# An attention and mixture-of-experts kernel: one subtraction in two instructions, new planner costs, and full-width products for one chunk in nine

## The chip, the cores and the metric

The kernel runs on one core of a Trainium2 chip. The metric is the device time of one execution in microseconds (us); the kernel before takes 906.83 us as the median of three runs (902.57 to 909.19). The engines that the text speaks of are TensorE (PE in the rows; PEld is its weight load), VectorE (DVE), ScalarE (ACT), GpSimd (POOL) and SyncE (SP), which issues most transfers. Each works through a queue of its own in order; semaphores tie them together.

## The reference

Attention over 4 batches, 8 heads, 1152 keys and 64 columns, with the queries averaged in pairs (576 per batch and head), and then a mixture of 8 experts of which each token takes two:

```python
q_pool = q.reshape(B, H, S // 2, 2, D).mean(axis=3)
scores = scale * np.matmul(q_pool, k.transpose(0, 1, 3, 2))
scores = scores - np.max(scores, axis=-1, keepdims=True)
attn = np.exp(scores)
attn = attn / (np.sum(attn, axis=-1, keepdims=True) + 1e-09)
x = np.matmul(attn, v)                       # then tokens x 512
noisy = x @ w_gate + np.log1p(np.exp(x @ w_noise)) * noise
top2 = np.argpartition(-noisy, 2, axis=1)[:, :2]   # softmax of the two: weights
out[mask] += top2_w[mask, k, None] * (np.maximum(x[mask] @ w1[e], 0) @ w2[e])
```

## The kernel before

**Attention.** The work is cut into 16 pairs (two batches of one head). A pair has 9 chunks of 128 queries; chunk 4 is mixed: its first 64 queries are of the first batch and its last 64 of the second. Three chunks make a segment, so there are 48 segments, and the middle segment of each pair (g = 1) holds the mixed chunk. A segment goes through 9 steps of 128 keys. Two steps make a unit, 216 in all.

For a unit, TensorE computes the scores (`score`, lines 342 and 343, two matmuls for each step and batch), ScalarE takes the exponential into a pair of buffers as 32-bit numbers `pf` (`exp`, line 350), and then P is split: the upper 16 bits of each number, read in place as bf16, are the high half `ph`, and `pl = pf - ph`, as f16, is the low half (`p_lo`, line 354). This subtraction is done by either GpSimd or VectorE, 140 and 76 times. The product with V (`pv`, line 370) takes both halves: for each step and chunk, three matmuls in which P is the stationary operand and V, with a column of ones that gives the row sum, is the moving one: ph with 65 columns of V's high half, ph with 64 of V's low half, pl with 65 of the high half. For the mixed chunk each of the three is done twice, with 64 stationary columns each, one time with each batch's V, into partitions 0 to 63 and 64 to 127 of the same PSUM columns. After the ninth step `evac` divides by the row sum (lines 381 to 383) on VectorE, and ScalarE and VectorE split the result into two f16 halves (388, 390).

Ahead of a pair's scores stand its loads, the splits of K, Q and V into halves (lines 281 on VectorE, 284 on ScalarE), transposing transfers, differences of keys (`kd`, line 291) and a pass that finds each query's maximum (scores on TensorE, line 297; ScalarE 305; VectorE 311 and 320). The PSUM has two wide tiles for scores and four banks; the banks serve the maximum pass, the products with V and the routing by turns. P has six buffer pairs.

**The planner.** The order of the attention's instructions on every queue is set at build time by `Plan`: each piece of work is an `op` with an engine, a booked duration, a due key, what it depends on and which buffers it takes. The planner walks a clock forward, holds an in-order queue for each engine (`LAT` is booked from a result to its reader, `GAP` between two works on an engine), and always writes out the op that can start first; within 0.25 us it takes the one with the smaller key. Works that use the SBUF port which VectorE and GpSimd share (`port=True`) are not booked at the same time. Where two engines are given, as for `p_lo`, it takes the one that would end first. The booked numbers decide the order and the split between engines; the chip runs that order with its own durations. For a step of P x V the op books 0.29 us, whether the segment is a middle one or not.

**After the attention.** The routing of the first 1152 tokens (`Route.steps`, lines 640 to 790: transposes, gate products, some 60 small VectorE instructions, then GpSimd's scatters, line 99) is planned inside the attention. The routing of the second half starts as segments end; its pieces that the plan hasn't placed by the attention's end are woven into `Moe.early`, which runs two experts on their first 256 tokens (matrix products 927 and 948, relu and its correction 936 and 937, weight splits 872 and 874). Then `Moe.run` takes the experts at full width, each after its tokens were fetched by a transposing transfer.

## Time and profile before

| | |
|---|---|
| median of three runs | 906.83 us (902.57 to 909.19) |
| the profiled execution | 906.73 us, of which 904.9 us span |
| TensorE busy, matmuls | 825.2 us (91%), 8686 matmuls |
| VectorE busy | 539.1 us (60%) |
| ScalarE busy | 445.4 us (49%) |
| GpSimd busy | 354.5 us (39%) |
| mean granted clock of TensorE | 0.975 |
| P x V (line 370) | 47 to 458 us |

A busy time is the union of an engine's instructions; matmuls overlap in a pipeline, so a row with 0.19 us for a matmul doesn't mean that the next starts only then, and how long a run of them takes is read from their start times. Shares over the whole span mix two parts: attention, where all engines work, and the experts, where TensorE is nearly always busy and the others aren't.

### The profile page before, as it was taken

The page shows a single profiled execution, that of the slowest core. Times are in us where ns is not written, and L with a number is a line of the kernel's source. Part 1 is how long each engine was busy: PE and PEld are TensorE (multiplying, and loading weights), DVE is VectorE, ACT ScalarE, POOL GpSimd, SP SyncE. Part 2 cuts the span into 40 slices and gives each one's busy share as a digit, 9 for nine tenths or more (in the row PEclk, how much of TensorE's full clock was granted, in tenths as well). Part 3 has the DMA queues.
Part 4 walks back from the last instruction along what each step waited for, and adds up shares of the span by engine and source line. Part 5 has one row for each costly group of instructions (what it writes and reads, how often), then busy time and mean ns, then how long its engine had stood idle before and what let it go on. Part 6 is the DMA issues. An engine that isn't in the chain of part 4 may idle for free.

```text
span 904.9 us, 21011 instructions
## 1 busy us (share of the span) xinstructions
PE 825.2 (91%) x8686; PEld 540.2 (60%) x8686; DVE 539.1 (60%) x1257; ACT 445.4 (49%) x663; POOL 354.5 (39%) x317
## 2 busy tenths in 40 slices
PE   3799899999999699789987799999999999999995
PEld 0367666767677566567774455757465565647542
DVE  4988887988899898898888133334323241422200
ACT  4678787767776466676534132333333332322310
POOL 4347577666762468755306501020211202020132
PEclk9889999999999799999999899999999999999998
DMA  8897986898699649574387936273836437281143
GB/s 195 204 245 166 202 212 178 179 216 182 153 219 184 172 106 215 130 204 98 109 166 258 255 43 165 65 220 84 209 71 172 108 106 176 71 212 22 24 51 44
DMA packets 213636, 137.79 MB, mean 152 GB/s; under 512 B 150304, under 2 KB 183584, under 8 KB 213536
## 3 DMA queue, kind: packets, MB, share of 16 engines
q1 hardware_dynamic: 204896, 116.33, 53.4%
q0 software_dynamic: 8640, 20.08, 11.4%
q8 instruction: 69, 1.13, 0.5%
q14 instruction: 31, 0.25, 0.1%
HBM read 62.14 MB, written 35.44 MB: 108 GB/s over the span
## 4 chain that ended last, share of the span: by engine, by line
PE 69%; DVE 17%; issue 6%; POOL 3%; DMA 3%; ACT 1%; SPq 1%; ACTq 0%; POOLq 0%; DVEq 0%
PE pss L927 21%; PE psm L948 20%; PE psm L370 13%; PE psm L297 6%; PE pss L342 5%; PE pss L343 5%; DVE pl L354 3%; DVE rd L311 3%; POOL xg L99 2%; DVE vv L281 2%; DVE mx L320 1%; DMA kr<-in_k_dram 1%; DVE kd L291 1%; DMA xT<-xg 1%; DVE rt L700 1%
## 5 line engine op out<-in xcount | busy, mean ns | idle before, releaser
L354 POOL TENSOR_TENSOR pl<-pf 128x768 f16<-128x768 f32 x140 | 223.8, 1610 | 148.6 <-ACT pf L350 140.4
L350 ACT ACTIVATE pf<-pss 128x768 f32<-128x768 f32 x216 | 173.9, 811 | 75.8 <-PE pss L343 67.1
L370 PE MATMUL psm<-vv,pf 128*128 128x65 f16 (+2 forms) x2880 | 188.8, 199 | 4.7 <-DVE vv L281 3.4
L370 PEld LDWEIGHTS <-pf 128*128 128x128 bf16 (+1 forms) x2880 | 156.0, 101 | 60.0 <-issue 20.5
L99 POOL DMA_INDIRECT out_dram<-y,mti x40 | 62.6, 1566 | 326.3 <-ACT y L953 316.6
L370 PE MATMUL psm<-vv,pl 128*128 128x65 f16 (+1 forms) x1440 | 176.3, 195 | 1.8 <-DVE pl L354 1.8
L343 PE MATMUL pss<-qt,kt 66*128 66x384 f16 (+1 forms) x576 | 149.9, 289 | 0.1
L342 PE MATMUL pss<-qt,kt 128*128 128x384 f16 (+1 forms) x576 | 149.3, 288 | 0.6 <-ACT pf L350 0.5
L937 DVE SCALAR_TENSOR_TENSOR hl<-pss,hh 128x640 f16<-128x640 f32 (+2 forms) x68 | 50.2, 738 | 159.0 <-ACT hh L936 159.0
L370 PEld LDWEIGHTS <-pl 128*128 128x128 f16 (+1 forms) x1440 | 127.9, 103 | 5.8 <-issue 3.7
L948 PE MATMUL psm<-wh,hl 128*128 128x512 f16 x320 | 121.3, 379 | 0.0
L948 PE MATMUL psm<-wl,hh 128*128 128x512 f16 x320 | 121.3, 379 | 0.0
L948 PE MATMUL psm<-wh,hh 128*128 128x512 f16 x320 | 121.3, 379 | 0.0
L936 ACT ACTIVATE hh<-pss 128x640 f16<-128x640 f32 (+2 forms) x68 | 43.2, 635 | 131.8 <-PE pss L927 131.8
L948 PEld LDWEIGHTS <-hh 128*128 128x128 f16 x640 | 62.4, 98 | 73.3
L311 DVE CUSTOM_DVE_ANT_0 rd<-psm,rd 128x512 f32<-128x512 f32 x144 | 96.7, 682 | 14.2 <-ACT rd L305 13.3
L305 ACT ACTIVATE rd<-psm 128x512 f32<-128x512 f32 x144 | 85.8, 597 | 36.9 <-PE psm L297 17.5
L953 ACT ACTIVATE y<-psm,mg 128x512 f32<-128x512 f32 x40 | 27.5, 687 | 151.2 <-issue 77.3
L297 PE MATMUL psm<-kt,qt 128*128 128x512 f16 (+3 forms) x320 | 78.3, 321 | 21.1 <-DVE mx L311 8.5
L927 PE MATMUL pss<-xT,fh 128*128 128x320 f16 (+1 forms) x448 | 85.7, 308 | 4.9 <-DMA xT<-xg 4.9
L354 DVE TENSOR_TENSOR pl<-pf 128x768 f16<-128x768 f32 x76 | 85.3, 1133 | 2.4 <-ACT pf L350 2.3
L927 PE MATMUL pss<-xT,wh 128*128 128x320 f16 (+1 forms) x448 | 83.4, 303 | 0.0
(157 smaller groups left out, 1170.3 us busy)
## 6 DMA issues: line engine op xcount, KB each, us to landing
xg<-zt SPq DMA_DIRECT2D x40, 260.0 KB, 5.3
kr<-in_k_dram SPq DMA_DIRECT2D x32, 288.0 KB, 3.7
vr<-in_v_dram SPq DMA_DIRECT2D x16, 576.0 KB, 4.6
kr<-in_moe_w_dram SPq DMA_DIRECT2D x17, 512.0 KB, 4.6
qr<-in_moe_w_dram SPq DMA_DIRECT2D x16, 512.0 KB, 4.3
kn<-in_moe_w_dram SPq DMA_DIRECT2D x16, 512.0 KB, 3.6
qr<-in_q_dram SPq DMA_DIRECT2D x31, 256.0 KB, 3.5
vr<-in_moe_w_dram SPq DMA_DIRECT2D x15, 512.0 KB, 5.3
```

Of the source, the lines that this page charges most:

```text
L99: i = nc.gpsimd.indirect_dma_start(out=out, out_offset=bass.IndirectOffsetOnAxis(ap=idx, axis=0), in_=src, in_offset=None, **kw)
L297: s.nc.tensor.matmul(ps[r, o:o + m.shape[1] * P], s.G.buf["qt", i][:, c, r], m, start=True, stop=True)
L305: s.nc.scalar.activation(s.G.buf["rd", i, c], s.G.buf["D", i, c], AF.Relu)
L311: s.nc.vector.tensor_tensor_reduce(out=rd, in0=s.G.buf["S", i, c], in1=rd, scale=1.0, scalar=-3.0e38, op0=ALU.add, op1=ALU.max, accum_out= ...
L342: mm(ps[:, a, o:o + w], kt[:, hh * NK + kc, :], qf[:, q0:q0 + w], start=True, stop=False)
L343: mm(ps[:, a, o:o + w], kt2[0:66, hh * NK + kc, :], qf2[0:66, q0:q0 + w], start=False, stop=True)
L350: s.nc.scalar.activation(s.parts(u)[0], s.G.buf["ps", u][:, :, 0:SG], AF.Exp, scale=0.125 / (IN_SCALE * IN_SCALE))
L354: (s.nc.vector if eng == "DVE" else s.nc.gpsimd).tensor_sub(pl, pf, ph)
L370: mm(ps[o:o + m, ci, 0:w], src[:, t % 2, ci * P + o:ci * P + o + m], vv[:, hh * NK + kc, a:b], start=st, stop=last and src is pl, skip_gro ...
L927: nc.tensor.matmul(ps[:, i, 0:N], w[:, dc, f * P:(f + 1) * P], xT[:, 2 * dc + x, i * N:(i + 1) * N], start=(n == 0), stop=(n == 11))
L937: s.nc.vector.scalar_tensor_tensor(hl, ps, 0.0, hh, op0=ALU.max, op1=ALU.subtract)
L948: nc.tensor.matmul(ps, h[:, f, b * P:(b + 1) * P], w[:, f, :], start=(n == 0), stop=(n == 23))
```

## The change

Three things are changed. `p_lo` on GpSimd becomes two instructions, one for each step of the unit (128 x 384 in place of 128 x 768); on VectorE it stays one. In `pv` the mixed chunk's three matmuls are done with all 128 stationary columns for both batches: with the first batch's V into the chunk's own PSUM columns, of which partitions 0 to 63 are used, and with the second batch's into 64 spare columns of the bank (`other`, columns 195 to 258), of which partitions 64 to 127 are used; the row sum needs no second copy, since it doesn't depend on V. `evac` has one more VectorE instruction for these 64 x 64 values, and its scratch columns move by 8. And the planner's booked durations are changed in nearly all ops. The core of the diff:

```diff
-    LAT = {"PE": 0.25, "ACT": 0.1, "DVE": 0.1, "POOL": 0.12, "SP": 4.0}
-    GAP = {"PE": 0.0, "ACT": 0.04, "DVE": 0.03, "POOL": 0.03, "SP": 0.05}
+    LAT = {"PE": 0.25, "ACT": 0.14, "DVE": 0.11, "POOL": 0.12, "SP": 4.0}
+    GAP = {"PE": 0.0, "ACT": 0.01, "DVE": 0.01, "POOL": 0.02, "SP": 0.05}
...
     def p_lo(s, u, eng):
         pf, ph, pl = s.parts(u)
-        (s.nc.vector if eng == "DVE" else s.nc.gpsimd).tensor_sub(pl, pf, ph)
+        if eng == "DVE":
+            s.nc.vector.tensor_sub(pl, pf, ph)
+            return
+        for a in range(2):
+            s.nc.gpsimd.tensor_sub(pl[:, a], pf[:, a], ph[:, a])
+
+    def other(s, n):
+        return s.G.buf["pv", n][:, 195:259]
...
-            parts = [(0, 0, 64), (1, 64, 64)] if c == 4 else [(int(c > 4), 0, P)]
             for src, a, b, w in ((ph, 0, 65, 65), (ph, 65, 129, 64), (pl, 0, 65, 65)):
-                for hh, o, m in parts:
+                for hh in (0, 1) if c == 4 else (int(c > 4),):
                     st = kc == 0 and ci == 0 and src is ph and a == 0
-                    mm(ps[o:o + m, ci, 0:w], src[:, t % 2, ci * P + o:ci * P + o + m], vv[:, hh * NK + kc, a:b],
+                    o = s.other(n) if hh and c == 4 else ps[:, ci]
+                    x = min(w, o.shape[1])
+                    mm(o[:, 0:x], src[:, t % 2, ci * P:ci * P + P], vv[:, hh * NK + kc, a:a + x],
                        start=st, stop=last and src is pl, skip_group_check=True)
...
             nc.vector.tensor_mul(xa, ps[:, :, 0:64], r.to_broadcast([P, 3, 64]))
+            if g == 1:
+                nc.vector.tensor_mul(xa[64:P, 1], s.other(n)[64:P], r[64:P, 1].to_broadcast([64, 64]))
             return
...
-            ex[u] = op("ACT", 0.82, 2 * u + 0.2, lambda u=u: s.exp(u), deps=[sc], take=[("pt", ("pt", u))], give=[("ps", u)])
-            pls[u] = op((("POOL", 1.5), ("DVE", 0.9)), 0, 2 * u + 2, lambda eng, u=u: s.p_lo(u, eng), deps=[ex[u]], port=True)
+            ex[u] = op("ACT", 0.71, 2 * u + 0.2, lambda u=u: s.exp(u), deps=[sc], take=[("pt", ("pt", u))], give=[("ps", u)])
+            pls[u] = op((("POOL", 1.43), ("DVE", 0.87)), 0, 2 * u + 2, lambda eng, u=u: s.p_lo(u, eng), deps=[ex[u]], port=True)
...
-                done.append(op("PE", 0.29, t + 8, lambda n=n, kc=kc: s.pv(n, kc), deps=[pls[t // 2]] + vdone[i] + done[-1:],
+                done.append(op("PE", 0.375 if n % 3 == 1 else 0.28, t + 8, lambda n=n, kc=kc: s.pv(n, kc), deps=[pls[t // 2]] + vdone[i], after=done[-1] if done else None,
```

The last pair of lines also lets a step of P x V be booked right behind the step before it on TensorE, where before it was booked only after that step's result time.

What the planner makes of it can be read from the built order. On TensorE, a middle segment's step around the mixed chunk (psm is the segment's bank, pf and pl the two halves of P, vv is V with its column of ones). Before, after a full-width chunk:

```order
L370 LDWEIGHTS pf_119
L370 MATMUL psm_66<-vv_128,pf_119 128x64
L370 LDWEIGHTS pl_120
L370 MATMUL psm_66<-vv_128,pl_120 128x65
L370 LDWEIGHTS pf_119
L370 MATMUL psm_66<-vv_128,pf_119 64x65
L370 LDWEIGHTS pf_119
L370 MATMUL psm_66<-vv_128,pf_119 64x65
L370 LDWEIGHTS pf_119
L370 MATMUL psm_66<-vv_128,pf_119 64x64
L370 LDWEIGHTS pf_119
L370 MATMUL psm_66<-vv_128,pf_119 64x64
```

And such a place now:

```order
L378 LDWEIGHTS pf_109
L378 MATMUL psm_66<-vv_128,pf_109 128x64
L378 LDWEIGHTS pl_110
L378 MATMUL psm_66<-vv_128,pl_110 128x65
L378 LDWEIGHTS pf_109
L378 MATMUL psm_66<-vv_128,pf_109 128x65
L378 LDWEIGHTS pf_109
L378 MATMUL psm_66<-vv_128,pf_109 128x64
L378 LDWEIGHTS pf_109
L378 MATMUL psm_66<-vv_128,pf_109 128x64
L378 LDWEIGHTS pf_109
L378 MATMUL psm_66<-vv_128,pf_109 128x64
```

The number of matmuls in the step is the same, twelve; the first number of a matmul's size is the count of output partitions, and all are 128 now. On GpSimd, the start of the attention before (qs is the sum of query pairs):

```order
L436 TENSOR_TENSOR qs_100<-qr 128x576 x2
L354 TENSOR_TENSOR pl_116<-pf_115 128x768
L354 TENSOR_TENSOR pl_118<-pf_117 128x768
L354 TENSOR_TENSOR pl_120<-pf_119 128x768
L436 TENSOR_TENSOR qs_100<-qr 128x576
```

And now:

```order
L446 TENSOR_TENSOR qs_100<-qr 128x576
L358 TENSOR_TENSOR pl_110<-pf_109 128x384 x2
L358 TENSOR_TENSOR pl_118<-pf_117 128x384 x2
L358 TENSOR_TENSOR pl_110<-pf_109 128x384 x2
L358 TENSOR_TENSOR pl_112<-pf_111 128x384 x2
L446 TENSOR_TENSOR qs_100<-qr 128x576
```

Each unit is two rows on end, and which units GpSimd takes has changed; over the whole program it takes 139 units where it took 140, and VectorE 77 where it took 76. On VectorE, the end of the attention before, from the last subtraction on (r and psm close a segment, wl is the low half of an expert's weight, ru and rt are the routing, hl is the correction of a relu):

```order
L390 TENSOR_TENSOR xr_84<-psm_67,xr_84 128x3x64
L381 TENSOR_SCALAR r<-psm_68 128x3
L382 RECIPROCAL r<-r 128x3
L383 TENSOR_TENSOR psm_68<-psm_68,r 128x192
L390 TENSOR_TENSOR xr_85<-psm_68,xr_85 128x3x64
L874 SCALAR_TENSOR_TENSOR wl_8041<-qr,wh_8040 128x1024
L675 TENSOR_SCALAR ru_7839<-psm_67 128x48
L680 SCALAR_TENSOR_TENSOR rt_8096<-ru_7839 128x24
L682 TENSOR_SCALAR rt_8096<-rt_8096 128x24
L937 SCALAR_TENSOR_TENSOR hl<-pss_64,hh 128x256
```

And now, from the close of the last segment on:

```order
L389 TENSOR_SCALAR r<-psm_67 128x3
L390 RECIPROCAL r<-r 128x3
L391 TENSOR_TENSOR psm_67<-psm_67,r 128x192
L400 TENSOR_TENSOR xr_85<-psm_67,xr_85 128x3x64
L884 SCALAR_TENSOR_TENSOR wl_8196<-qr,wh_8195 128x1024
L947 SCALAR_TENSOR_TENSOR hl<-pss_64,hh 128x256
L884 SCALAR_TENSOR_TENSOR wl_8196<-kn,wh_8195 128x1024
L947 SCALAR_TENSOR_TENSOR hl<-psm_66,hh 128x256
L884 SCALAR_TENSOR_TENSOR wl_8196<-kr,wh_8195 128x1024
L685 TENSOR_SCALAR ru_8008<-psm_68 128x48
L690 SCALAR_TENSOR_TENSOR rt_8287<-ru_8008 128x24
L692 TENSOR_SCALAR rt_8287<-rt_8287 128x24
```

The first row of the second half's routing stands behind one weight split before, and behind three weight splits and two relu corrections now.

## Rows read from the trace of the kernel before

**Rows 1.** Busy us (and instructions) by engine in five stages; granted clock, DMA.

```profile
47.00:300.00 253.00, 237.64 (x3759) 175.89 (x3759) 216.13 (x467) 189.31 (x293) 157.83 (x100) 0.99 0.88 196
300.00:400.00 100.00, 84.04 (x1234) 61.81 (x1233) 90.59 (x230) 61.47 (x95) 70.39 (x68) 0.93 0.68 166
400.00:458.00 58.00, 55.43 (x981) 44.45 (x978) 49.49 (x85) 37.32 (x55) 22.28 (x13) 0.97 0.45 102
458.00:516.00 58.00, 45.71 (x410) 31.12 (x407) 38.72 (x222) 20.21 (x36) 27.16 (x44) 1.00 0.82 242
516.00:905.00 389.00, 377.25 (x2208) 216.84 (x2207) 110.78 (x178) 111.82 (x148) 59.35 (x73) 0.98 0.48 109
```

The columns are start and end, length, PE, PEld, DVE, ACT, POOL, then the granted clock of TensorE, the share of DMA and GB/s.

**Rows 2.** Chain of waits from 47 to 458 us, shares by engine and line.

```profile
by line: PE psm L370 27.6%; PE psm L297 11.5%; PE pss L342 10.4%; PE pss L343 10.3%; issue 8.2%; DVE pl L354 5.3%; DVE rd L311 4.7%; DVE vv L281 3.1%; DVE mx L320 2.3%; DVE kd L291 1.8%; DMA kr<-in_k_dram 1.2%; DVE rt L700 1.2%; DVE kn L281
```

**Rows 3.** Timeline of TensorE, a middle segment's step: start, us, engine, line, operation.

```profile
137.09 0.23 PE L370 MATMUL psm<-vv,pf 128*128 128x65 f16 x2
...
137.28 0.26 PE L370 MATMUL psm<-vv,pf 128*64 128x65 f16 x4
...
137.50 0.23 PE L370 MATMUL psm<-vv,pf 128*128 128x65 f16 x2
...
137.60 0.38 PE L297 MATMUL psm<-kd,qt 128*128 128x512 f16 x1
```

**Rows 4.** The same timeline, an ordinary step of P x V.

```profile
139.71 0.22 PE L370 MATMUL psm<-vv,pf 128*128 128x65 f16 x2
...
139.99 0.33 PE L342 MATMUL pss<-qt,kt 128*128 128x384 f16 x1
```

**Rows 5.** Shortest, middle and longest ns of a line's instructions; last, one small GpSimd group.

```profile
L354 POOL TENSOR_TENSOR pl<-pf x140: 1458/1469/2361, 29.2 to 449.3; 128x768 f16<-128x768 f32 x140
L354 DVE TENSOR_TENSOR pl<-pf x76: 942/950/2784, 29.2 to 456.3; 128x768 f16<-128x768 f32 x76
L281 DVE SCALAR_TENSOR_TENSOR kn<-kr,kn x32: 741/1084/3662, 5.0 to 381.6; 128x576 f16<-128x576 f32 x32
L281 DVE SCALAR_TENSOR_TENSOR vv<-vr,vv x17: 745/1473/2618, 33.0 to 437.4; 128x1152 f16<-128x1152 f32 x15, 128x576 f16<-128x576 f32 x2
L291 DVE TENSOR_TENSOR kd<-kt x32: 404/733/2456, 9.7 to 391.7; 128x512 f16<-128x512 f16 x32
L598 POOL IOTA ev<- 128x8 f32 x1 | 0.1, 133 | 0.0
```

**Rows 6.** Timelines of VectorE and GpSimd at 65 us.

```profile
65.12 2.02 DVE L281 SCALAR_TENSOR_TENSOR qn<-qs,qn 128x576 f16<-128x576 f32 x1
...
65.06 1.47 POOL L354 TENSOR_TENSOR pl<-pf 128x768 f16<-128x768 f32 x1 [2.23 <-ACT pf L350]
```

**Rows 7.** Pieces of the whole chain of waits: start, us, what (twelve such).

```profile
99.68 2.22 DVE pl L354
...
440.78 2.15 DVE pl L354
```

**Rows 8.** Waits from 60 to 440 us; then two groups of the page.

```profile
POOL pl L354 <- ACT pf L350: 126.1, 74, 6.8
...
PE psm L297 <- DVE mx L311: 13.4, 11, 4.7
...
L354 POOL TENSOR_TENSOR pl<-pf 128x768 f16<-128x768 f32 x140 | 223.8, 1610 | 148.6 <-ACT pf L350 140.4
L350 ACT ACTIVATE pf<-pss 128x768 f32<-128x768 f32 x216 | 173.9, 811 | 75.8 <-PE pss L343 67.1
```

**Rows 9.** The chain of waits from 440 to 520 us.

```profile
458.48 0.38 DVE psm L383
...
479.95 0.99 POOL xg L99
...
509.11 7.25 DMA xT<-xg
```

**Rows 10.** Small route steps on VectorE, 440 to 520 us: count, busy us, mean ns.

```profile
L700 DVE SCALAR_TENSOR_TENSOR rt<-rt,rt 128x24 f32<-128x24 f32 x18 | 3.1, 172 | 0.1
```

More of the change, by code (lines that the diff above doesn't have):

```diff
@@ L418, in pairs @@
             for h, c in enumerate(hs):
-                hi = op("ACT", 0.69, k(50, 90) + 4 * h, lambda i=i, c=c: s.hi(B["kn", i][:, c, 0:D], B["kr", i][:, c], scale),
+                hi = op("ACT", 0.58, k(50, 90) + 4 * h, lambda i=i, c=c: s.hi(B["kn", i][:, c, 0:D], B["kr", i][:, c], scale),
                         deps=[lk[h]], take=[("kn", ("kn", i)), ("kt", ("kt", i))] if h == 0 else (), after=hi)
-                lo = op("DVE", 0.73, k(48, 90) + 4 * h,
+                lo = op("DVE", 0.67, k(48, 90) + 4 * h,
                         lambda i=i, c=c: s.lo(B["kn", i][:, c, D:], B["kr", i][:, c], scale, B["kn", i][:, c, 0:D]),
@@ L444, in q_hi @@
                          B["qs", i][:, c, None, :].to_broadcast([P, m, 2, D]), 0.5 * scale)
-                hi = op("ACT", 0.2 + 0.96 * f, k(44, 91) + 8 * p * x, q_hi, deps=[a])
+                hi = op("ACT", 0.1 + 0.96 * f, k(44, 91) + 8 * p * x, q_hi, deps=[a])
                 t = op("SP", 1.35, k(43, 91) + 8 * p * x, lambda i=i, c=c: s.transpose(B["qt", i][:, c], B["qn", i][:, c]), deps=[hi], lat=2.7,
@@ L460, in pairs @@
                     c = 3 * g + ci
-                    mm = op("PE", 0.44, k0 + 3 * ci, lambda i=i, c=c: s.max_mm(i, c),
+                    mm = op("PE", 0.62 if c == 4 else 0.43, k0 + 3 * ci, lambda i=i, c=c: s.max_mm(i, c),
                             deps=[df[h] for h in w] + [q],
                             take=[("bank", ("D", i, c)), ("bank", ("S", i, c))], give=[("kd", i)])
-                    rl = op("ACT", 0.61, k0 + 3 * ci + 0.5, lambda i=i, c=c: s.max_relu(i, c), deps=[mm],
+                    rl = op("ACT", 0.48, k0 + 3 * ci + 0.5, lambda i=i, c=c: s.max_relu(i, c), deps=[mm],
                             take=[("rd", ("rd", i, c))], give=[("D", i, c)])
-                    red.append(op("DVE", 0.78, k0 + 3 * ci + 1, lambda i=i, c=c: s.max_red(i, c), deps=[rl],
+                    red.append(op("DVE", 0.67, k0 + 3 * ci + 1, lambda i=i, c=c: s.max_red(i, c), deps=[rl],
                                   give=[("S", i, c), ("rd", i, c)]))
-                rest = op("PE", 0.17, k0 + 5, lambda i=i, g=g: s.max_rest(i, g), deps=red, take=[("bank", ("R", i, g))])
-                red.append(op("DVE", 0.57, k0 + 7, lambda i=i, g=g: s.rest_red(i, g), deps=[rest], give=[("R", i, g)]))
+                rest = op("PE", 0.39 if g == 1 else 0.17, k0 + 5, lambda i=i, g=g: s.max_rest(i, g), deps=red, take=[("bank", ("R", i, g))])
+                red.append(op("DVE", 0.47, k0 + 7, lambda i=i, g=g: s.rest_red(i, g), deps=[rest], give=[("R", i, g)]))
                 allred += red
@@ L483, in pairs @@
             for h, c in enumerate(vs):
[L484 removed]
+                hi = op("ACT", 0.1 + 0.96 / len(vs), b + 3 * h, lambda i=i, c=c: s.hi(B["vv", i][:, c, 0:D], B["vr", i][:, c], scale),
                         deps=[lv], take=[("vv", ("vv", i))] if h == 0 else (), after=hi)
[L486 removed]
+                vdone[i].append(op("DVE", 0.08 + 1.2 / len(vs), b + 3 + 6 * h,
                                    lambda i=i, c=c: s.lo(B["vv", i][:, c, 65:129], B["vr", i][:, c], scale, B["vv", i][:, c, 0:D]),
```

16 lines of the change are left out of this document (7 added, 9 removed).

## The prediction

> **What bounds the kernel now.** I first cut the span into stages by what runs in them. From 516 us on, TensorE is busy for 377 of 389 us with the experts' matrix products, at a granted clock of 0.98 [rows 1]; nothing of the diff touches that code, so these 389 us stay. What the change can move lies before. All P x V products (line 370) lie between 47 and 458 us, and in these 411 us three engines are all nearly full: between 47 and 300 us TensorE is busy for 237.6, VectorE for 216.1 and GpSimd for 157.8 of 253 us [rows 1]. From 300 to 400 us, where the routing of the first half of the tokens runs on VectorE, VectorE has 90.6 of 100 us and TensorE falls to 84.0, its granted clock to 0.93. So no single engine is the bound: the reader should see a ring of three in-order queues that wait for each other by turns.
>
> The chain of waits over 47 to 458 us says which of them ends last: P x V (L370) 27.6%, the other three TensorE lines together 32.2%, VectorE's lines 18.4% as far as the row goes (pl 5.3, rd 4.7, vv 3.1, mx 2.3, kd 1.8, rt 1.2; kn is cut off behind), and 8.2% in which nothing is named [rows 2]. GpSimd's subtraction is not on the row, and GpSimd waits 126.1 us for the exponential in the 380 us from 60 to 440, the largest wait of that stretch, while TensorE waits 13.4 us for VectorE's running maximum [rows 8]. A slower GpSimd is thus hidden; a shorter P x V and a VectorE that is held up less are not.
>
> **The mixed chunk's products.** A step of ordinary P x V is nine matmuls; the one from 139.71 to 139.99 us takes 0.28 us, 0.031 each [rows 4]. A step of a middle segment has twelve, six of them with 64 stationary columns, and takes from 137.09 to 137.60, 0.51 us [rows 3]. Inside it the six half-wide ones take 0.22 (137.28 to 137.50), 0.037 each, so half the columns are not cheaper; the rest of the difference stands at the two changes of width. With 128 columns throughout, twelve times 0.031 is 0.37 us. The count of matmuls stays, the 64-column forms disappear (the order shows them as 128-wide rows). There are 16 middle segments of 9 steps, 144 in all, so TensorE has 144 x 0.14 = 20 us less to do. That is not yet time. All of P x V is 288 x 0.28 + 144 x 0.51 = 154 us, and the chain holds 27.6% of 411 = 113 us of it, 0.74. I take 0.74 x 20 = **-15 us**; the bounds are 0 (each step was waiting anyway) and -20.
>
> **The subtraction in halves.** One GpSimd instruction over 768 elements takes 1.458 us at least, and the same on VectorE 0.942 [rows 5]. The two do not overlap: at 65.06 us GpSimd starts one and ends at 66.53; VectorE's subtraction for q starts at 65.12 and takes 2.02 us [rows 6] where the shortest of that shape in line 281 takes 0.741 [rows 5]. It stood still for 1.28 us, until GpSimd's instruction was nearly over. The same shows in the spread of VectorE's own forms: kd from 0.404 to 2.456 us, kn from 0.741 to 3.662, pl from 0.942 to 2.784 [rows 5]. On the chain I find twelve such pieces over 1.4 us (pl, vv, kn, kd, rt), the first at 99.68 and the last at 440.78 us, and without each form's shortest (for vv, which has two shapes, its middle) some 14 us remain, 1.2 us a piece [rows 5, 7]. With GpSimd's instruction at half the length VectorE can wait for at most half as long, some 0.6 us, provided it is let in between the halves. That saves about 0.6 x 12 = **-7 us**. The bounds: nothing (the second half goes first), and -10 (the shorter stalls that I didn't list shrink too).
>
> What it costs: 139 units now have one more GpSimd instruction each. No row shows a 384-element one. Below, it costs nothing (half of 1.458 is 0.73); above, all of the 0.133 us that an instruction of 8 elements takes there [rows 5] comes on top once per unit, which makes 18 us on GpSimd. Either sits behind the 126 us in which GpSimd waits for ACT [rows 8]; where GpSimd works several units on end it lengthens their holding of the port, for which I book **+1 us** (0 to +5). [...]
>
> The second half also carries waits of its own in the built order, on TensorE's and often on GpSimd's semaphore: they guard the pair's earlier use, six units back. The exponential that writes the same pair has waited for those readers already, so I book nothing; were one late, the next units on GpSimd would queue behind it, and P x V behind them.
>
> **The extra multiplication.** 16 segments get one more VectorE instruction of 64 x 64 from PSUM. It lies between the 0.17 us of a small route step [rows 10] and the 0.38 us of the 128 x 192 one that it follows [rows 9], say 0.2 us: 3 us on VectorE, on the chain's share of VectorE **+1 us** (0 to +3).
>
> **The planner's numbers.** They move no work but its order. A mixed step was booked at 0.29 us where it takes 0.51; over 144 steps the plan ran 32 us ahead of TensorE, and everything ordered against it (when a maximum is reduced, when a bank comes free) stood early. It is now booked at 0.375, near my 0.37. The exponential drops from 0.82 to 0.71, under the 0.81 that its row has as the mean [rows 8], with 0.14 in place of 0.10 to its reader. A step of P x V is no longer booked 0.25 behind the result of the step before, so steps of a segment can stand closer. No row prices an order that has not run. The bound on both sides is half of TensorE's idle time in the three stages of attention (15.4 + 16.0 + 2.6 us [rows 1]), 17 us; I take a tenth of the 32 us, **-3 us**.
>
> At one place the order can be priced. After the last P x V product at 458 us, VectorE closes the last segments, and the routing of the second half starts: its first scatter begins at 479.95, 21.9 us later [rows 9], and from there GpSimd's scatters run on end up to the transfer that the next expert waits for, so a later first scatter is paid in full. Before, the first route step stands behind one weight split; now behind three splits and two relu corrections. Counted from the last subtraction, the row that makes the first scatter's rows ready is the 119th before and the 141st now: 22 rows, mostly of the 0.17 us kind [rows 10], **+4.5 us** (0 to +6, since VectorE is not full in these first microseconds).
>
> **Sum.** -15 - 7 + 1 + 1 - 3 + 4.5 = -18.5 us. The profiled execution took 906.7 us (span 904.9 and 1.8 around it), the median of the three runs is 906.8, so no shift between them: 888 us.
>
> **The rivals.** *The ring closes elsewhere (about 903 us).* TensorE gets its 20 us, but the next wait, VectorE's, ends at the same time: between 300 and 400 us VectorE is at 90.6% already. Then only the stalls count, -7 + 1 + 1 + 4.5 - 3, which is -3.5 us, 903. Against it: P x V is the largest item of the chain, and the mixed steps are a third of the steps in every stage.
>
> *GpSimd keeps the port (about 895).* If the second half begins before a waiting VectorE instruction is let in, the halves act as one: the -7 falls away. One kn reaches 3.662 us [rows 5], 2.92 over its shortest, which is two GpSimd instructions on end, so it happens. The other pieces of the chain stay under one such instruction plus their own work, or near it. [...]
>
> *GpSimd falls behind (about 923, slower).* The plan books 1.43 us for a unit of two instructions where one alone takes 1.458 at least and 1.61 on average with its stalls [rows 5, 8]. If a unit costs 0.13 more and meets stalls as now (0.15), it takes 0.3 us longer than booked, and the products that read it stand in TensorE's queue ahead of the next scores. That turns once GpSimd's backlog outlives its waits for ACT; if TensorE then loses 0.25 us for each of the 139 units, it is +35 us, 906.7 - 18.5 + 35 = 923. Against it: GpSimd's waits for ACT are a third of the 380 us.
>
> *The plan comes true (about 874).* With all durations near the trace, the whole 17 us of idle time comes back, 14 more than booked: 888 - 14 = 874. For it: the 32 us by which the plan was out. Against it: part of the idle time is VectorE's own load between 300 and 400 us.
>
> **How the numbers follow.** My forecast, 878 to 898: 0.50, of which 0.10 is the kept port. The plan comes true, under 878: 0.22. The ring closes elsewhere, 898 to 916: 0.20. GpSimd falls behind, above 916: 0.08. A range with 8 in 10 reaches from 868 to 908. About 1% (9 us) is what a measurement of this kernel can tell from no change. Faster by more than that: 0.73; within it: 0.19; slower: 0.08.
>
> **What would show it.** A mixed step at 0.37 to 0.38 us between its first matmul and what follows, with no 64-column form under line 370's successor. GpSimd's halves at 0.73 to 0.80 us where nothing holds them up. The long tails of kd, kn and pl on VectorE ending near their minimum plus 0.7 us. The last P x V at about 435 us (458 less 23, the sum without the routing) in place of 458. The first scatter of the second half 25 to 27 us behind it. The experts from the first wide one on unchanged at 389 us. I am wrong if P x V's end stays near 458 while TensorE's wait for VectorE or GpSimd grows, or if TensorE waits for GpSimd's halves at all, which it doesn't now.

## The result, and the profile after

The kernel after takes 895.46 us (median of four runs, 891.53 to 897.22); the kernel before, run beside it, 907.15. The ratio is 0.9889 with a 95% interval of 0.9857 to 0.9921, so it is faster by 1.1%, and the time lies 7.5 us above the forecast of 888, in the range of 868 to 908. The profiled execution took 897.22 us, of which 895.3 us span:

```profile
PE 811.7 (91%) x8686; PEld 533.7 (60%) x8686; DVE 532.5 (59%) x1276; ACT 444.2 (50%) x663; POOL 395.9 (44%) x453
```

The same five stages as in [rows 1], cut at the same events of this execution (columns as there):

```profile
47.00:300.00 253.00, 236.36 (x3817) 176.81 (x3816) 223.90 (x516) 195.23 (x303) 196.28 (x202) 0.98 0.93 205
300.00:400.00 100.00, 83.78 (x1246) 60.23 (x1244) 91.81 (x232) 65.43 (x102) 75.47 (x95) 0.93 0.62 156
400.00:439.00 39.00, 37.03 (x758) 31.96 (x757) 35.88 (x59) 24.81 (x36) 15.83 (x14) 1.00 0.59 130
439.00:507.00 68.00, 48.77 (x413) 32.31 (x410) 37.94 (x223) 20.64 (x36) 26.01 (x43) 0.89 0.82 214
507.00:895.00 388.00, 376.85 (x2208) 216.74 (x2207) 110.88 (x178) 111.84 (x148) 60.54 (x75) 0.98 0.46 108
```

Three cuts give the balance of these two executions. The last P x V product comes at 439.0 us, where before it came at 457.8: 18.8 us gained in the attention. From there to the first wide expert product it now takes 68.2 us, where it took 58.6: 9.6 us lost. The experts take the same time within half a microsecond. In the first stage VectorE is now busy for 223.9 of 253 us (216.1 before), and GpSimd for 196.3 (157.8): each 100 us hold more work of both.

The mixed step, as TensorE's timeline shows it now (the answer to [rows 3]); L378 is the new number of the line of P x V:

```profile
134.31 0.22 PE L378 MATMUL psm<-vv,pf 128*128 128x65 f16 x2
134.37 0.19 PE L378 MATMUL psm<-vv,pl 128*128 128x65 f16 x1
134.40 0.28 PE L378 MATMUL psm<-vv,pf 128*128 128x65 f16 x4
134.52 0.22 PE L378 MATMUL psm<-vv,pl 128*128 128x65 f16 x2
134.58 0.23 PE L378 MATMUL psm<-vv,pf 128*128 128x65 f16 x2
134.65 0.19 PE L378 MATMUL psm<-vv,pl 128*128 128x65 f16 x1
134.67 0.22 PE L378 MATMUL psm<-vv,pf 128*128 128x65 f16 x2
```

Twelve matmuls start between 134.31 and the next step at 134.67: 0.36 us, where it was 0.51. The forms with 64 stationary columns are gone.

Shortest, middle and longest duration of the lines that share the port (the answer to [rows 5]; L358 and L355 are now the subtraction on GpSimd and on VectorE):

```profile
L358 POOL TENSOR_TENSOR pl<-pf x278: 817/827/1939, 27.4 to 437.9; 128x384 f16<-128x384 f32 x139
L355 DVE TENSOR_TENSOR pl<-pf x77: 943/951/2469, 31.2 to 436.3; 128x768 f16<-128x768 f32 x77
L281 DVE SCALAR_TENSOR_TENSOR kn<-kr,kn x32: 746/858/2465, 5.5 to 367.8; 128x576 f16<-128x576 f32 x32
L291 DVE TENSOR_TENSOR kd<-kt x32: 410/426/2391, 9.6 to 379.8; 128x512 f16<-128x512 f16 x32
```

A half takes 0.817 us, more than half of 1.458; so a unit takes at least 1.634. The middle kd falls from 0.733 to 0.426 us and the middle kn from 1.084 to 0.858: at least half of the kd now meet next to no stall. The middle of VectorE's own pl stays (0.950 and 0.951), and the longest values stay near 2.4 us. No row names the port itself, which is the planner's word (`port=True`). What the traces show is that these works take longer beside GpSimd's subtraction: before, kn takes 0.747 to 0.759 us in the ten that lie beside none and up to 3.662 in the 22 that do, while line 383, which works on a bank of the PSUM, takes 0.365 to 0.367 in all 48.

The page's row of GpSimd's subtraction (its row of before is in [rows 8]: 223.8 us busy, 1610 ns each):

```profile
L358 POOL TENSOR_TENSOR pl<-pf 128x384 f16<-128x384 f32 x278 | 268.7, 996 | 101.6 <-ACT pf L350 90.6
```

A unit is now 1.99 us on average where it was 1.61. The 120 halves that lie beside no work of VectorE on pl, kd, kn, qn, vv or qs take 0.817 to 0.892 us, and the 158 that do up to 1.939: GpSimd's halves are also held up by VectorE between them.

The waits from 60 to 420 us (the answer to [rows 8]):

```profile
POOL pl L358 <- ACT pf L350: 67.2, 34, 5.5
...
PE psm L297 <- DVE mx L311: 8.5, 12, 2.3
```

GpSimd's wait for the exponential falls from 126.1 us (in 380) to 67.2 (in 360); about half of its slack is used. TensorE waits for GpSimd's halves for 4.1 us in all, in six waits, where it didn't wait before.

The tail after the last product, from GpSimd's timeline and then from the chain (the answer to [rows 9]):

```profile
466.37 0.99 POOL L99 DMA_INDIRECT xg<-xr,rt  x1 [26.88 <-DVE rt L739]
...
492.53 1.61 POOL out_dram L99
...
494.20 12.87 DMA xT<-xg
...
507.12 7.89 PE pss L937 x32
```

The first scatter starts 27.4 us behind the last product (22.1 before, counted from 457.8), and the transposing transfer ahead of the first wide expert takes 12.87 us where it took 7.25.

### The profile page after: what moved, and what is told of

It is laid out like the page before. It is cut to its first block, busy times and chain, and to the rows that moved or that the text cites. A ratio compares the mean times of both kernels' runs of the same rounds, so it can differ in the third digit from the quotient of the medians.

```text
span 895.3 us, 21230 instructions
## 1 busy us (share of the span) xinstructions
PE 811.7 (91%) x8686; PEld 533.7 (60%) x8686; DVE 532.5 (59%) x1276; ACT 444.2 (50%) x663; POOL 395.9 (44%) x453
## 4 chain that ended last, share of the span: by engine, by line
PE 44%; POOL 2%; DMA 2%; DVE 1%; issue 1%; ACT 0%; POOLq 0%; ACTq 0%
PE pss L937 22%; PE psm L958 21%; POOL xg L99 1%; DMA xT<-xg 1%; PE psm L937 1%; POOL out_dram L99 0%; DMA xTg<-xr 0%; DVE wl L884 0%; PE psm L681 0%; ACT y L963 0%; DVE rt L730 0%; POOL sp L97 0%; DVE rt L748 0%; DVE hl L947 0%; DVE rt L710 0%
## 5 line engine op out<-in xcount | busy, mean ns | idle before, releaser
L358 POOL TENSOR_TENSOR pl<-pf 128x384 f16<-128x384 f32 x278 | 268.7, 996 | 101.6 <-ACT pf L350 90.6
L378 PEld LDWEIGHTS <-pf 128*128 128x128 bf16 x2880 | 157.8, 98 | 47.9 <-issue 18.2
L378 PE MATMUL psm<-vv,pf 128*128 128x65 f16 (+1 forms) x2880 | 168.2, 195 | 2.3 <-DVE kd L291 0.8
L378 PE MATMUL psm<-vv,pl 128*128 128x65 f16 (+1 forms) x1440 | 159.6, 194 | 2.7 <-POOL pl L358 1.8
L378 PEld LDWEIGHTS <-pl 128*128 128x128 f16 x1440 | 127.6, 100 | 3.3 <-POOL pl L358 2.2
L355 DVE TENSOR_TENSOR pl<-pf 128x768 f16<-128x768 f32 x77 | 88.3, 1160 | 0.0
```

What stands on the lines that cost most here:

```text
L355: s.nc.vector.tensor_sub(pl, pf, ph)
L358: s.nc.gpsimd.tensor_sub(pl[:, a], pf[:, a], ph[:, a])
L378: mm(o[:, 0:x], src[:, t % 2, ci * P:ci * P + P], vv[:, hh * NK + kc, a:a + x], start=st, stop=last and src is pl, skip_group_check=True)
```

## Experiments: the two edits, each alone and both, in the old order

The first question was whose the gain is. In three kernels the edits were put on the kernel before with its booked durations left as they were, so that every queue has the order of before but for the edited instructions. Each time below is a median, and each ratio is to the kernel before on the same chip, which took 905.3 to 906.3 us in these comparisons.

**Products alone.** The mixed chunk's full-width products, with `other` and the extra multiplication, and nothing else:

```diff
-            parts = [(0, 0, 64), (1, 64, 64)] if c == 4 else [(int(c > 4), 0, P)]
...
-                for hh, o, m in parts:
+                for hh in (0, 1) if c == 4 else (int(c > 4),):
...
```

> The kernel before with one part alone: the mixed chunk's products with 128 stationary columns (and the extra 64 x 64 multiplication). Booked durations are those of before, so every queue's order is that of before. Theory A (TensorE's own work ends last: each microsecond taken from it comes through, its idle time stays): the mixed step falls from 0.51 to 0.37 us, the last P x V moves from 458 to 438-441 us, the time is 886 to 890 us. Theory B (the prediction's ring: only three quarters of it lie on the path): last P x V at 443-446 us, 891 to 895 us. Rival C (VectorE and GpSimd are the bound): 900 us or more.

902.93 us (897.35 to 909.14), ratio 0.9964 [0.9937, 0.9992]: 3.3 us, where TensorE has 144 x 0.15 = 22 us less to do; it is the third of the cases expected. The chain of waits of this kernel, from 48 to 454 us, by line (the answer to [rows 2]; L374 is P x V):

```profile
by line: PE psm L374 15.3%; issue 10.3%; PE psm L297 9.1%; DVE pl L354 7.9%; DVE rd L311 7.7%; PE pss L343 7.7%; PE pss L342 7.6%; DMA kr<-in_k_dram 3.8%; DVE vv L281 3.1%; DVE kd L291 3.0%; DVE mx L320 2.4%; DVE kn L281 2.4%; POOL pl L354 
```

P x V's share falls from 27.6 to 15.3%, and what takes its place is mostly VectorE: pl from 5.3 to 7.9, rd from 4.7 to 7.7, kd from 1.8 to 3.0. The chain has re-formed, in the main through VectorE, the next engine of the ring.

**Halves alone.** GpSimd's subtraction in two instructions on the kernel before:

```diff
-        (s.nc.vector if eng == "DVE" else s.nc.gpsimd).tensor_sub(pl, pf, ph)
+        if eng == "DVE":
+            s.nc.vector.tensor_sub(pl, pf, ph)
+            return
+        for a in range(2):
+            s.nc.gpsimd.tensor_sub(pl[:, a], pf[:, a], ph[:, a])
```

> The kernel before with one part alone: the subtraction on GpSimd in two instructions; the order on every queue is that of before. Theory A (a half takes 0.82 us, so that a unit costs 0.18 more on GpSimd, and this gives back what the shorter stalls of VectorE save): 904 to 911 us, VectorE's stalls fall by a quarter, GpSimd's busy time grows by 40 us, last P x V within 3 us of 458. Theory B (the prediction: the shorter stalls save 7 us on the path): last P x V at 450-453 us, 899 to 902 us. Rival C (GpSimd becomes the bound): last P x V beyond 462 us, over 912 us.

894.72 us (890.2 to 898.51), ratio 0.9893 [0.9861, 0.9925]: 11.5 us, as much as the whole change gives, and more than the best of the cases expected (899 to 902 us).

**Both, in the old order.**

> The kernel before with the mixed chunk's full-width products and the split subtraction, but with the booked durations of before: the changed kernel without its new order. Theory A: as the full-width products alone, 886 to 891 us, so that the new order cost 4 to 8 us against it, most of it behind the last P x V. Theory B (the new order gave 3 us in the attention and cost 4.5 behind it): 892 to 896 us. Rival C (the new order is where the gain is): 900 us or more.

885.17 us (881.93 to 885.92), ratio 0.9780 [0.9753, 0.9807]. It is the fastest kernel of the study, the two edits with the numbers of the old plan, and a little faster than the best case expected.

The busy times from the start to the last P x V product in each execution show where the attention's time goes (columns as in [rows 1]). Before, products alone, halves alone, both in the old order, and after:

```profile
0.00:458.00 458.00, 402.26 (x6072) 292.30 (x6073) 389.60 (x857) 313.36 (x479) 268.01 (x200) 0.97 0.78 178
```

```profile
0.00:455.00 455.00, 392.47 (x6073) 291.40 (x6074) 396.56 (x874) 312.21 (x479) 269.36 (x200) 0.95 0.77 179
```

```profile
0.00:445.00 445.00, 399.71 (x6064) 290.13 (x6064) 373.84 (x857) 312.92 (x479) 314.39 (x340) 0.98 0.79 183
```

```profile
0.00:437.00 437.00, 384.56 (x6074) 287.03 (x6075) 381.69 (x874) 311.90 (x479) 318.12 (x341) 0.96 0.80 186
```

```profile
0.00:439.00 439.00, 386.06 (x6071) 284.64 (x6072) 383.64 (x876) 311.76 (x479) 309.36 (x336) 0.97 0.82 185
```

Behind the length stands TensorE's busy time, and two columns on VectorE's. With the products alone TensorE falls by 9.8 us, and VectorE rises by 7.0, of which the 16 new multiplications are 3.9 (0.242 us each): the end moves by 3. With the halves alone VectorE falls by 15.8 us and the end moves by 13. VectorE's busy time holds its stalls beside GpSimd (61 us before and 46 after, below), and its queue, works and stalls together, fills 84 to 87% of the attention in each of the five. TensorE fills 86 to 90%, so neither is the limit alone. Each row is one execution, and the end of the attention differs by some 7 us between executions of one order (below).

TensorE's clock moves too. The traces of before and after have it at two levels, a granted clock of 1.00 and one of 0.50: before, the first wide expert's 128x384 products start 0.32 us apart at 517 us, where the granted clock is 0.50, and 0.16 apart from 522.6 us on, where it is 1.00. In these five traces TensorE was granted the lower one for 31, 44, 20, 38 and 27 us of the time up to the last P x V product. With the products alone that is 14 us more than before. At the halved pace these do some 7 us less work (an estimate, half of the difference), which is a part of why TensorE's busy time fell by 9.8 and not by 22 us. Over all runs the median granted clock is 0.972 before, 0.9675 with the products alone, 0.9785 with the halves alone and 0.971 with both. So a part of what each edit brought or lost may have come through the clock; no run here separates it.

In the old order the two edits bring more together than each alone: the products are worth 3.3 us without the halves and 9.5 with them (894.72 to 885.17), and the halves 11.5 and 17.8 us (902.93 to 885.17).

## Experiments: why the halves help

**Cut another way.** Halves can help in two ways: VectorE gets the port between them, or the first half's step can be taken by TensorE earlier. Cut across the queries, each instruction holds a part of both steps, and the second chunk of the first step reads both, so that step can't run through before the second is done; the port comes free as often:

```diff
...
+        for a in range(2):
+            r = slice(a * 192, a * 192 + 192)
+            s.nc.gpsimd.tensor_sub(pl[:, :, r], pf[:, :, r], ph[:, :, r])
```

> The kernel before with the subtraction on GpSimd in two instructions of the same size as in split_only, but cut across the queries (2 x 192) and not between the two steps: the second chunk of the first step reads both halves, so P x V cannot start earlier than with one instruction. Orders as before. Theory A (the halves help because VectorE waits for the port half as long): 892 to 898 us as with split_only (894.7), last P x V at 443-448 us. Theory B (they help because the first step's products can start 0.8 us earlier): 903 to 910 us, last P x V at 454-460 us.

895.35 us (892.69 to 898.93), ratio 0.9887 [0.9868, 0.9907], the first of the cases expected, against 894.72 of the halves by steps. The earlier step is worth nothing that can be told, which leaves the port. In the trace of after the two engines' timelines show it:

```profile
91.79 1.04 DVE L291 TENSOR_TENSOR kd<-kt 128x512 f16<-128x512 f16 x1
92.76 1.58 DVE L355 TENSOR_TENSOR pl<-pf 128x768 f16<-128x768 f32 x1
```

```profile
91.51 2.01 POOL L358 TENSOR_TENSOR pl<-pf 128x384 f16<-128x384 f32 x2 [1.45 <-PE psm L378]
```

GpSimd's two halves start at 91.51, and a key difference on VectorE at 91.79, which takes 1.04 us where the shortest takes 0.41: a stall of 0.63. It ends at 92.83, and the two halves on GpSimd run until 93.52, so it was let in between them. VectorE's own subtraction behind it takes 1.58, again 0.64 over its shortest. Summed over VectorE's works that share the port (pl, kd, kn, qn, vv, qs), each less the shortest of its shape, the stalls up to the last P x V product are 61 us before, 61 with the products alone, 44 with the halves alone, 45 with the cut across the queries, 48 with both and 46 after. They don't account for the time by themselves: from the products alone to both they fall by 13 us, and the time by 17.8.

**Quarters.** If shorter instructions are better, four of 192 elements should be better still, unless their own cost eats it:

```diff
...
+        for a in range(4):
+            r = slice(a % 2 * 192, a % 2 * 192 + 192)
+            s.nc.gpsimd.tensor_sub(pl[:, a // 2, r], pf[:, a // 2, r], ph[:, a // 2, r])
```

> Both parts with the booked durations and orders of before (885.2 us), the subtraction on GpSimd now in four instructions of 192 elements. If a half's 0.82 us against 1.46 for the whole means 0.18 us a piece for the instruction itself, a quarter takes 0.50 and a unit 1.99 us, 350 us for 140 units. Theory A (VectorE's stalls are what costs, their length goes with the instruction): stalls fall from 48 to some 30 us and the time to 878-883 us. Theory B (GpSimd, now at 350 of 440 us, is late itself, and products wait for it): 890 us or more. In between, 884 to 888 us: the two cancel.

898.21 us (893.56 to 901.43), 13.0 us slower than the same kernel with halves, and the second of the cases expected. The line's durations, and the waits from 60 to 430 us:

```profile
L359 POOL TENSOR_TENSOR pl<-pf x560: 497/504/1637, 30.5 to 443.7; 128x192 f16<-128x192 f32 x187
```

```profile
POOL pl L359 <- ACT pf L350: 23.6, 10, 6.1
...
PEld L379 <- POOL pl L359: 15.6, 38, 1.2
...
PE psm L379 <- POOL pl L359: 9.6, 24, 1.1
```

A quarter takes 0.497 us, a unit at least 1.99. GpSimd's slack is nearly gone, and TensorE waits for it for 25 us. On the chain of waits from 48 to 448 us GpSimd's subtraction is now the largest item with 18.6%, where with halves (48 to 436 us) it has 2.7%. VectorE's stalls go no lower than 43 us. This is the rival "GpSimd falls behind", reached one cut later than its place in the prediction.

**More units on VectorE.** The plan books a unit on GpSimd at 1.5 us (1.43 in the new numbers), and it takes 1.634 or more. Booked near that, the planner gives VectorE more of the units: 93 in place of 76 with the old numbers, 103 in place of 77 with the new.

```diff
-            pls[u] = op((("POOL", 1.5), ("DVE", 0.9)), 0, 2 * u + 2, ...
+            pls[u] = op((("POOL", 1.66), ("DVE", 0.9)), 0, 2 * u + 2, ...
```

> Both parts with the booked durations of before but one: 1.66 us for a unit on GpSimd in place of 1.5; the planner gives GpSimd 123 units and VectorE 93, against 140 and 76. Theory A (an order booked nearer to the chip is better): 878 to 883 us. Theory B (17 more units on VectorE, the fuller engine, cost): 888 to 896 us. Theory C: 884 to 887 us.

> The changed kernel with one number changed: a unit of two halves on GpSimd is booked at 1.66 us, near the 0.82 a half takes, in place of 1.43. The planner then gives GpSimd 113 units and VectorE 103, against 139 and 77. Theory A (the new order lost because it booked GpSimd too short): 886 to 891 us. Theory B (VectorE is the fuller engine, and 26 more units of 0.95 us on it cost): 898 to 908 us. Theory C (no matter): 893 to 897 us.

With the old numbers 898.98 us (894.17 to 901.43), 13.8 over the same kernel with 1.5; with the new ones 917.37 us (910.97 to 920.6), ratio 1.0151 [1.0104, 1.0198], 22 over after. Both are slower than the slowest case expected (896 and 908 us). The attention of these two, old numbers first:

```profile
0.00:451.00 451.00, 388.54 (x6082) 287.40 (x6082) 393.01 (x891) 313.55 (x479) 287.64 (x309) 0.96 0.77 181
```

```profile
0.00:459.00 459.00, 390.52 (x6073) 284.85 (x6074) 403.19 (x900) 313.03 (x479) 274.46 (x287) 0.97 0.78 177
```

VectorE's 11 us more (393.0 to 381.7) put the end of P x V 14 us later, and 20 us more (403.2 to 383.6) put it 20 us later, while GpSimd has less to do and TensorE at most 4.5 us more. A duration booked nearer to the chip made the kernel slower, most likely because the planner moves work onto an engine that was nearly full already. These runs change the order too, so they fit a VectorE that has no room and don't price a microsecond of it.

## Experiments: what the new plan costs

**New plan alone.** The booked durations and the order of after, with the products and the subtraction of before:

> The changed kernel's booked durations and order alone: half-width products for the mixed chunk (0.51 us where 0.375 is booked) and the subtraction in one instruction. With it the two parts stand by two plans: before, 906.3, 902.9 (products), 894.7 (halves), 885.2 (both); new plan, this, 902.8 (products), 895.5 (both). Theory A (the new order costs some 10 us wherever the halves are in, and nothing without): 904 to 909 us. Theory B (the new order is worse throughout, and products hide it): 912 to 918 us. Theory C (the new order is better by itself): under 902 us.

910.15 us (906.83 to 916.25), ratio 1.0060 [1.0034, 1.0086]: 4.0 us slower than before, between the first two of the cases expected.

**After with the subtraction in one instruction:**

```diff
...
-        for a in range(2):
-            s.nc.gpsimd.tensor_sub(pl[:, a], pf[:, a], ph[:, a])
+        s.nc.gpsimd.tensor_sub(pl, pf, ph)
```

> The changed kernel with the subtraction on GpSimd in one instruction again; booked durations and so the order on every queue are those of the changed kernel. Theory A (the halves give nothing): within 3 us of the changed kernel, 891 to 898 us, with VectorE's stalls a quarter longer and GpSimd's busy time 40 us less. Theory B (the halves save 7 us): 900 to 904 us. Rival C (the halves cost, since GpSimd is late): 886 to 890 us.

902.83 us (898.34 to 908.01), ratio 0.9974 [0.9951, 0.9997], the same as the products alone in the old order (902.93), and the second of the cases expected. So in the new order the halves bring 7.4 us with the products in, where in the old one they bring 17.8. The traces suggest a reason: VectorE's stalls are 54 us with the plan alone and 51 in this kernel, where the old order has 61, and the halves bring them to 46; the new order leaves less for them to take. The products bring 7.3 us here without the halves (910.15 to 902.83), where in the old order they bring 3.3, so they don't need the halves in every order. The fourth kernel of the new order, the halves without the products, was not run.

The new plan thus costs 4.0 us without either edit, 0 with the products, and 10.3 with both (895.46 against 885.17). Where it does so, in pairs of executions:

| | last P x V | to the first wide expert product | first scatter behind the last P x V |
|---|---|---|---|
| before / plan alone | 457.8 / 456.8 | 58.6 / 64.8 | 22.1 / 27.6 |
| products alone / after, one instruction | 454.7 / 447.2 | 59.5 / 64.2 | 22.6 / 27.7 |
| both in the old order / after | 436.6 / 439.0 | 59.0 / 68.2 | 22.7 / 27.4 |

The first scatter is 5 us later in each pair, and the tail, from the last P x V to the first wide expert product, 5 to 9 us longer. It is the place that the order showed: the first route step of the second half stands behind three weight splits and two relu corrections.

**The output's scatters held back.** In after, the transposing transfer ahead of the first wide expert is slow, 12.87 us (494.20 to 507.08). In the trace, the 256-byte packets of that transfer run among the 2048-byte packets of the output's scatters, which start at 492.53 us, as GpSimd comes free of the routing: from 496 to 505 us some 320 of the small ones start in each microsecond, and 1130 from 507 us on, where no large ones are left. In before such packets lay beside the first 4 us of the transfer, which took 7.25 us. The loads of the first two wide experts' tokens are moved ahead of the scatters, and two small copies on GpSimd make the scatters wait until both transposes have landed:

```diff
-        for e in range(2):
-            s.xload(e, EARLY, CAP)
...
+            for e in range(2):
+                M.xload(e, EARLY, CAP)
+            for e in range(2):
+                nc.gpsimd.tensor_copy(M.hold[:, e:e + 1], M.X[e, EARLY][0:1, 0, 0:1])
             M.put()
             M.run()
```

> The changed kernel (895.5 us) with the same hold: the first four scatters into the output wait until both transposing transfers have landed. Theory A (these scatters' packets among the transposes' make 12.9 us of the 7.1 from issue to first wide matmul): 5.5-7.5 us there, 888 to 891 us. Theory B (the long transposes have another cause, the order or the weights' transfers): 11-13 us there, 894 to 897 us.

> Both parts with the booked durations of before (885.2 us), and GpSimd's first four scatters of expert rows into the output made to wait, by a tiny copy that reads them, until the two transposing transfers for the first wide experts have landed. Theory A (the scatters' packets slow the transposes wherever they run side by side): the span from the transposes' issue to the first wide matmul falls from 7.1 to 5-6 us, 883 to 885 us. Theory B (no contention): 885 us or later.

In after with the hold the transfer comes down to 5.12 us:

```profile
498.23 4.14 DMA xg<-xr,rt
...
502.58 5.12 DMA xT<-xg
...
507.74 7.30 PE pss L938 x30
```

But the time is 895.49 us (890.33 to 898.65), as before the hold, and in the old order 886.06 (883.57 to 889.37) against 885.17. The transfer in after came out as the first of the cases expected, the times of both kernels as the second. The contention is real where it was seen, and taking it away is worth nothing that the medians show. One execution of after was profiled, so whether the transfer is as slow in each isn't known. In the execution with the hold the last P x V came at 445.8 us where it came at 439.0 in after, by the same order of the attention; the pair in the old order shows the same (443.6 and 436.6), and there the medians of the two kernels differ by only 0.9 us. TensorE was at its lower clock for 34 us of the attention with the hold and 27 without, and 41 and 38 in the old order. One profile's end of the attention is thus good to some 7 us.

**The routing released earlier.** The leftover routing pieces were given to the early experts' weave 3 us sooner:

```diff
-return [[max(0.0, o.ready - G.now), o.gen, PACE] for o in G.can]
+return [[max(0.0, o.ready - G.now - 3.0), o.gen, PACE] for o in G.can]
```

> The changed kernel (895.5 us) with one edit: what the plan leaves of the second half's routing is released 3 us earlier behind the attention, so that its first VectorE row stands behind one weight split again, as before the change, and not behind three. The attention's order is that of the changed kernel. Theory A (the new order's cost lies in this row's place: first scatter 27.4-27.8 us after the last P x V in the four kernels with the new order so far, 22.1-22.7 in the six with the old): 22-24 us there, 889 to 892 us. Theory B (it lies in the attention): 894 to 897 us.

The first scatter moves from 27.4 to 25.1 us behind the last product, and the kernel takes 894.46 us (892.4 to 895.85), ratio 0.9899 [0.9862, 0.9935]. That is 1 us under after and inside the spread. The scatter was expected 22 to 24 us behind, as in the old order, and came back only half of the way, so this run is not a full test of the row's place.

What stays open: how the 10.3 us of the new plan divide. The tail is longer in all six profiles with the new order (61.9 to 68.2 us, against 58.4 to 60.4 in the kernels with the old one), which makes some 5 us of it likely; the rest lies in the attention, where the halves find fewer stalls to take, and the 7 us between executions hide how much it is. Neither of the two attempts at the tail brought the time down.

## Why the prediction held, and where its terms were off

The direction, the range and the band given to the forecast (878 to 898) held. The sum came out 7.5 us too low, and the terms tell why. In the change's own order, by the one path that was run, there stand: the plan alone +4.0 us where +1.5 was booked, the products with their multiplication -7.3 where -14, the halves with their cost -7.4 where -6. The products' term is the one that was mis-sized most; the plan's comes next.

- **The products, -15 us: mis-sized.** The step was priced rightly: 0.36 us measured where 0.37 was said. What failed is the factor 0.74, the part of P x V that the chain of before held. A share of a chain says what ends last now; it doesn't say how far the next engine is behind. Alone, the products gave 3.3 us in the old order and 7.3 in the new, and 9.5 with the halves in. The 3.3 is close to the rival "the ring closes elsewhere", whose mechanism was seen: the chain moved to VectorE. The clock may have taken another part, which the prediction left out: in the old order its median fell with them from 0.972 to 0.9675. The rival's price (903 for the whole change) did not come, since it gave the products nothing and both edits in the new order brought 14.7 us.
- **The halves, -7 us: right in the change's own order, too small in the old one.** The mechanism was right: a waiting VectorE gets in between the two, and 0.63 us is what it waits. In the new order the halves brought 7.4 us. In the old one they brought 11.5 alone and 17.8 with the products in, beyond the bound of -10, and VectorE's stalls fell by 13 to 17 us. So the count of twelve long stalls on the chain of before, which is of the old order, was too narrow a base, and that -7 fits the new order is in part luck: that order had taken some of the stalls away by itself, which no term said.
- **Both together.** Products, halves, the half's cost and the extra multiplication were booked at -20 us. In the old order they measured -21.1, and the two errors cancelled; in the new order they measured -14.7.
- **The half's cost.** 0.817 us lies just outside the 0.73 to 0.80 that was to be seen. With the three lengths 768, 384 and 192 (1458, 817, 497 ns) the line is 176 ns for the instruction and 1.67 ns for an element, so the upper bound of 0.133 us was no bound. That is 24 us more on GpSimd. Its busy time with these subtractions rose by 45 us (223.8 to 268.7): the rest is mostly time in which its halves stand still for VectorE (beside VectorE's works its subtractions lie 48.8 us over their shortest in sum, and 20.9 before), a cost that the prediction didn't list. The 45 us are nearly all hidden behind GpSimd's waits for the exponential, as was argued (126 to 67 us). The extra multiplication takes 0.242 us, where 0.2 was said. A fixed part in every instruction told one cut further: quarters lose 13 us against halves.
- **The planner's numbers, -3 us: wrong sign in the whole.** The plan alone costs 4.0 us, and 10.3 with both edits in. In the attention the sign can't be told (1 us and 7.5 us earlier in two pairs, 2.3 later in the third). The tail's part was placed well: +4.5 us was booked for the later first scatter, and it came 5 us later in every pair, and 27.4 us behind the last product where 25 to 27 were said. The tail as a whole lost 5 to 9 us, the most in the change itself, where the slow transfer adds to it. The rival "the plan comes true" did not come: booked durations nearer to the trace won nothing, and the truer price of GpSimd's unit lost 14 and 22 us.
- **GpSimd keeps the port: did not come in the main.** Five of VectorE's works still stood through two halves or four (below). The other 115 that lie beside a half in the trace of after are at most 0.73 us over the shortest of their shape: the kd at 91.79 us stalls for 0.63 us beside two halves on end.
- **GpSimd falls behind: not at halves.** TensorE waits 4.1 us for them, where the prediction said that any such wait would prove it wrong; that sign was set too sharply.
- **The other signs.** The last P x V at 439 us (435 was said), the experts at 388 us (389), no 64-column form. The long tails of VectorE's works don't end at the shortest plus 0.7 us: kd still reaches 2.391 and pl 2.469. The middle values of kd and kn, which I should have named, are what fell.

## What to carry to other kernels

Where two engines hold up each other's works, as GpSimd and VectorE do here (kn takes 0.741 to 3.662 us before), try cutting the instructions of the one that has slack, as long as the cost of the cuts, with the time that it then stands still itself, fits in that slack: halves paid here and quarters cost. Whether VectorE's own subtraction should be cut as well was not run. The share of a chain of waits that a line has overstated here what speeding it up brings (15 us said, 3.3 to 9.5 measured); look for the engine that is next, and at the granted clock. Two edits on different engines of a ring can bring more together than the sum of each alone (21.1 and 14.8 us in the old order). Booked durations nearer to the chip are no gain in themselves when a list scheduler uses them to divide work: measure the edit with the old order and with the new one.

## What the runs showed of the hardware that was not expected

- GpSimd's subtraction of a bf16 array from a 32-bit one has a fixed part of 176 ns and 1.67 ns for an element (1458, 817 and 497 ns for 768, 384 and 192 elements in each partition).
- In the trace of after a waiting VectorE is mostly let in behind a GpSimd instruction, also when the next one is ready: 115 of its 120 works that lie beside a half are at most 0.73 us over the shortest of their shape. Five were not let in: they stood through two halves (at 339.77, 343.04, 347.70 and 367.83 us) or four (at 371.10, where VectorE's subtraction for q took 3.89 us). All five lie where the routing's scatters run on GpSimd too; the trace of both edits in the old order has five as well, between 325 and 374 us. Why is open.
- What VectorE no longer waits is in part waited on the other side: a unit of two halves takes 1.99 us on average, 0.36 over its shortest, where one instruction was 0.15 over.
- A transposing transfer took 12.87 us among the output's scatters, 7.25 before, where their packets lay beside its first 4 us only, and 5.12 without them.
- Executions of one and the same order of the attention end P x V up to 7 us apart (436.6 and 443.6; 439.0 and 445.8), while the experts that follow stay between 385 and 389 us.
